# A three-stage kernel whose instruction order is planned by a program: how three planning rules are changed

## The chip, the cores and the metric

The kernel runs on one core of one Trainium2 chip. The metric is the device time of one execution in microseconds (us); the median of a few runs is compared. TensorE (PE in the profile) multiplies matrices into PSUM, VectorE (DVE) and ScalarE (ACT) work element by element, GpSimd (POOL) does a little, and SyncE (SP) issues most DMAs. Each engine executes its own instructions strictly in the order in which they stand, and waits at the first one whose inputs or buffers are not ready.

## The reference, cut to what matters

Three layers follow each other over 4 sequences of 768 positions: a chunked scan with decays (8 heads, 32 values, state of 16), a gated feed-forward layer (256 to 1536 to 256) behind an RMS norm, and a second one (256 to 1024 to 256) that mixes each position with the one before.

```python
cum = np.cumsum(la, axis=-1)                       # la = log(clip(a)), in a chunk
M = CB * np.exp(cum_i - cum_j) * causal            # CB = C @ B^T, the "scores"
y = M @ x + (C @ state) * np.exp(cum)
state = decay_full * state + sum_j(B_j x_j * decay_from_j)
...
xn = x / rms * rms_g
x = (silu(xn @ w_gate) * (xn @ w_val)) @ w_out     # silu(g) = g * sigmoid(g)
...
k = np.maximum(xk @ w_k, 0); out = sigmoid(xr @ w_r) * (k * k @ w_v)
```

## The kernel before, in words

Time is cut into 6 chunks (`NC`) of 128 positions (`P`), each with all 4 sequences (`NB`): 512 columns (`T`). Chunk 0 of the scan stands alone ahead of everything. Then, in tile `t`, the first feed-forward layer of chunk `t` (`ffn1`, 12 units of gate `g`, value `v`, product `hf`, contraction into `x2`) runs with the scan of chunk `t + 1` between its units, and the second layer (`ffn2`) of chunk `t - 1` follows. Every wide product is three matmuls of 512 columns on values split into a high and a low part (`mm3`, L615 to L617): ScalarE rounds the high part (`split`, L128) and VectorE subtracts it for the low part (L131). The weights arrive as 64-bit numbers and are turned into such pairs in `convert` during the first two tiles, by ScalarE (L255, L256, L276) and VectorE (L260, L265, L267, L277).

In the scan, the decay matrices `E` of chunks 0 and 1 are made on chip: `sums_e` gets the cumulated logs, the matmuls `cumt` (L338) turn them into `cum`, `spread_e` spreads them over a bank `Eb` (L346, L347) and ScalarE's `exp_e` takes 4 exponentials of 128 columns from each bank (L116). `scores` multiplies B and C into two banks `sc` (L441 for chunks 0 and 1 on rows 0 to 31 and 32 to 63 of the array, one half of the rows for each bank; L448 for chunk 2 on rows 0 to 15 and 32 to 47; L454, on all rows, for the later ones). `mask` (L473) multiplies `sc` with `E` on VectorE and so frees the banks. `y_two` (L515, L486, L492) makes the output and state of two sequences in two banks. The scans `la_scan` (L399) and `e_scan` (L408) prepare the decays for the state and for later chunks.

PSUM has eight banks: 2 of `pacc` (tag "acc"), 4 of `pmm` ("mm": `g`, `v`, `kp`, `ss`), 2 of `patt` ("at": `sc`, `y`, and `Eb` from chunk 1 on). The order in which instructions stand on each engine comes from `Order`: it plays the program through with a price for every instruction (`price`) and a model of the waits, always gives a free engine the earliest written instruction that `can` run, and `arrange` ties every instruction behind the one ahead of it on its engine. `can` asks whether a tile that is first touched here has its turn and a free buffer. `chains` are extra pairs "this before that". The prices set only the order: what an instruction takes on the chip is another matter.

Of the kernel before, what the change touches and what calls it, by code (L numbers as in the profile page):

```python
# [16 lines left out]
P = 128  # L17
# [50 lines left out]
def tile_kernel(ctx: ExitStack, tc, a_c, x_t, B_t, B_s, C_s, B_p, C_p, C_h, kc,  # L68
                w_gate, w_val, w_out, w_k, w_v, w_r, out):
    nc = tc.nc  # L70
    slots, chains = {}, []

    class Pool:
        def __init__(self, name, bufs, space=None):
# [253 lines left out]
    def sums_e(a_sb):  # L328
        nc.vector.memset(f32(sums), 0.0)
        ln = t2("ln")[:RE]  # L330
        tabled(out=ln, in_=a_sb[:RE], func=AF.Ln)
        nc.vector.tensor_tensor_scan(out=ln, data0=starts.rearrange("p h i -> p (h i)"), data1=ln, initial=0.0,
                                     op0=ALU.mult, op1=ALU.add)
        nc.vector.tensor_copy(sums[:RE], ln)
        nc.vector.tensor_tensor(out=sums[32:32 + RE], in0=ln, in1=f32(sums[:RE]), op=ALU.subtract)
        ps = patt.tile([P, T], F32, tag="at", name="cumt")[:, :4 * RE].rearrange("p (h r) -> p h r", h=4)
        for h in range(4):
            nc.tensor.matmul(ps[:, h], sums[:, h * P:(h + 1) * P], pick, start=True, stop=True)  # L338
        nc.vector.tensor_scalar(out=cum, in0=ps, scalar1=-1.0, scalar2=None, op0=ALU.mult)

    def spread_e(c, b):
        for half in range(2):
# [20 lines left out]
    def parity(c):  # L363
        return c == 2
# [62 lines left out]
    def scores(c, b):  # L427
        d = A[c]
        bank = []
        for _ in range(2):  # L430
            if c == 0:
                pool, tag = pacc, "acc"
            else:
                pool, tag = patt, "at"
            bank.append(pool.tile([P, T], F32, tag=tag, name="sc"))
        if plain(c):
            br, cr = d.pop(("Br", b)), d.pop(("Cr", b))
            for q in range(2):
                for half in range(2):
                    g = slice(32 * half, 32 * half + 32)  # L440
                    nc.tensor.matmul(bank[half][:, q * 256:(q + 1) * 256], br[g, q, :],  # L441
                                     cr[g, 2 * q:2 * q + 2, :].rearrange("p a i -> p (a i)"), start=True, stop=True)
        elif parity(c):
            br, cr = d.pop(("Br", b)), d.pop(("Cr", b))
            for p in range(4):
                for j in range(2):
                    g = slice(32 * j, 32 * j + N)
                    nc.tensor.matmul(bank[j][:, p * P:(p + 1) * P], br[g, p, :], cr[g, p, :], start=True, stop=True)  # L448
        else:
            bs, cs = d.pop(("Bs", b)), d.pop(("Cs", b))  # L450
            for half in range(2):
                for q in range(2):
                    p = 2 * half + q
                    nc.tensor.matmul(bank[half][:, q * 256:(q + 1) * 256], bs[:, p, :],  # L454
                                     cs[:, p, :, :].rearrange("p a i -> p (a i)"), start=True, stop=True)
        for half in range(2):
            d["sc", b, half] = bank[half]
        if plain(c) and c or parity(c):
            load_bc(c, b + 2)
# [49 lines left out]
    def y_two(c, b):  # L509
        d = A[c]  # L510
        y = [patt.tile([P, T], F32, tag="at", name="y") for _ in range(2)]
        for k in range(2):
            for half in range(2):
                g = slice(64 * half, 64 * half + 64)
                nc.tensor.matmul(y[half][:, k * P:(k + 1) * P], Sf[g, b + k].rearrange("p h d -> p (h d)"),  # L515
                                 d["Ch"][g, b + k, :], start=k == 0, stop=False, skip_group_check=True)
        for k in range(2):
            y_x(y, (k * P, k * P), c, b + k, False)
            if c + 1 < NC:
                d["up", b + k] = y[k][:, 2 * P:2 * P + 2 * D]  # L520
                y_st(d["up", b + k], c, b + k)
        if b == 0:
            d["yT"] = rp.tile([P, 2, T], F32, tag="yT", bufs=1, name="yT")
        for half in range(2):
            nc.scalar.copy(d["yT"][:, half, b * P:(b + 2) * P], y[half][:, :2 * P])
        for k in range(2):
            st_up(c, b + k)
            sf_up(c, b + k)
# [223 lines left out]
        w_load()  # L752
    first, second = steps(), steps()
    clip(a_sb)
    sums_e(a_sb)
    spread_e(0, 0)
    scores(0, 0)
    spread_e(0, 1)
    for b in range(NB):
        for half in range(2):  # L760
# [145 lines left out]
        held[t] = x2  # L906
    mix(NC - 1, held.pop(NC - 1), act_e, vec_e)
    ffn2(NC - 1, lambda *_: None)
    arrange(tc, list(nc.cur_bb.bb.instructions), slots, chains)

# [15 lines left out]
class Order:  # L928
    SIGNAL, LANDING, RATE = 90.0, 1900.0, 270.0

    def __init__(self, instructions, slots, chains):
        self.slots, self.ins = slots, []
        where = {}
        for i in instructions:
            kind = type(i).__name__
            if i.engine in ENGINES and kind not in ("BassTilePoolBoundary", "InstRegisterMove"):
                where[i.name] = len(self.ins)
                self.ins.append(i)
        n = len(self.ins)
        self.eng = [i.engine for i in self.ins]  # L940
        self.before = [set() for _ in range(n)]
        for a, b in ((where[a], where[b]) for a, b in chains):
            self.before[b].add(a)
        self.tiles, self.touch = [[] for _ in range(n)], {}
        writes, reads = {}, {}
        for k, i in enumerate(self.ins):
            rs, ws = ([self.region(a, slots) for a in s if hasattr(a, "bass_ap")] for s in (i.ins, i.outs))
            for name, r in rs + ws:
                if name in slots and name not in self.tiles[k]:
                    self.tiles[k].append(name)  # L950
                    self.touch.setdefault(name, []).append(k)
            for name, r in rs:
                self.meet(k, r, writes.get(name, ()))
            for name, r in ws:
                self.meet(k, r, writes.get(name, ()))
                self.meet(k, r, reads.get(name, ()))
            for store, them in ((writes, ws), (reads, rs)):
                for name, r in them:
                    if slots.get(name, ("",))[0] == "PSUM":
                        store = writes  # L960
                    store.setdefault(name, []).append((r, k))
        self.cost = [self.price(i) for i in self.ins]
# [22 lines left out]
    def price(self, i):  # L985
        kind, e = type(i).__name__, i.engine
        aps = [a for a in i.outs if hasattr(a, "bass_ap")]
        n = max([columns(a) for a in aps] or [1])
        if kind == "InstDMACopy":
            return (380.0 if e == SP_ else 100.0), 0.0, False  # L990
        if e == PE_:
            x = i.ins[0]
            if x.dtype == F32:
                part = 0.3 if aps[0].ap[0][1] <= 32 else 0.55 if x.ap[0][1] <= 64 else 1.0
                return 20 + 1.7 * n * part, 200.0, False
            return (228.5 if n >= T else max(n / 2.4 + 15, 45.0)), 180.0, False
        if e == ACT_:
            return (1280.0, 0.0, False) if kind == "InstLoadActFuncSet" else (75 + 0.88 * n, 70.0, False)
        two = kind == "InstTensorTensor" or getattr(i, "is_scalar_tensor_tensor", False)
        if e == POOL_:  # L1000
            return (100 + 2.3 * n, 50.0, True) if kind == "InstTensorTensor" else (100 + 0.5 * n, 50.0, False)
        if kind == "InstMemset":
            return 60.0, 30.0, False
        psum = any(self.slots.get(a.bass_ap.tensor.name, ("",))[0] == "PSUM" for a in i.ins if hasattr(a, "bass_ap"))
        if getattr(i, "is_tensor_tensor_scan", False):
            return 20 + 2.22 * n, 70.0, True
        return 75 + (1.03 if two or psum else 0.52) * n, 75.0, not psum

    def run(self):
# [20 lines left out]
        t, serial, order, held, holder = 0.0, 0, [], set(), None  # L1030

        def can(k):
            return all(m in held or m in first.get(k, ()) and rank[m] == turn[self.slots[m][1]]
                       and free[self.slots[m][1]] > 0 for m in self.tiles[k])

        def release(j):
            left[j] -= 1
# [70 lines left out]
        return t, order  # L1108


def arrange(tc, instructions, slots, chains):
    o = Order(instructions, slots, chains)
    _, order = o.run()
    last = {}
    for k in order:
        i = o.ins[k]
        if i.engine in last:
            tc.add_manual_dep(i, last[i.engine].name, mybir.DependencyInfo(
                mybir.DependencyClass.NoSync, mybir.DependencyReason.DATA), reason="order")
        last[i.engine] = i  # L1120
# [38 lines left out]
```

## Time and profile before

| what | value |
|---|---|
| median of 3 runs (lowest, highest) | 542.84 us (542.33, 543.45) |
| the profiled execution's own time | 542.75 us |
| its span, first to last instruction | 541.0 us |
| TensorE busy in the span | 530.0 us (98%) |
| VectorE busy | 403.1 us (75%) |
| ScalarE busy | 315.0 us (58%) |
| mean granted TensorE clock | 0.986 of full speed |

The 1.75 us between own time and span lie around the instructions. Matmuls overlap in the pipeline, so that a busy TensorE row is longer than the distance to the next matmul; distances between starts are the truer measure there, and on VectorE too, where a following instruction starts before the end that is shown.

### The profile page before, as it was taken

How to read it: one execution, taken by the hardware profiler on the slowest of the kernel's cores; microseconds unless marked ns; L12 is line 12 of the kernel's file. 1: busy time of each engine (PE TensorE's matmuls, PEld its weight loads, DVE VectorE, ACT ScalarE, POOL GpSimd, SP SyncE). 2: the span in 40 equal slices, each digit the busy share in tenths (PEclk: the TensorE clock that was granted, in tenths of full speed). 3: DMA queues.
4: the chain of work that ended last, by engine and by line, in shares of the span. 5: the costliest groups of instructions: out<-in, count | busy, mean ns of one | idle time of the engine just before them, and what ended most of it. 6: DMA issues, size and time to landing. Idle time of an engine off the chain costs nothing.

```text
span 541.0 us, 7496 instructions
## 1 busy us (share of the span) xinstructions
PE 530.0 (98%) x2831; PEld 421.4 (78%) x2831; DVE 403.1 (75%) x640; ACT 315.0 (58%) x546; POOL 14.4 (3%) x30
## 2 busy tenths in 40 slices
PE   8979999999999999999999999999999999999997
PEld 5646777787778888888888888888887888888885
DVE  5797889999999986596986597986454873335672
ACT  3998557954745864355774356774337662345562
POOL 4000000000002000001000001000000000000000
PEclk9987999999989999999999999999999999999999
DMA  8552456533426011316011315011000010000001
GB/s 261 157 179 93 170 166 220 199 89 113 131 59 184 32 41 39 117 43 184 29 39 40 117 44 171 1 40 39 1 0 2 1 39 1 0 0 1 18 22 39
DMA packets 21635, 42.20 MB, mean 78 GB/s; under 512 B 2064, under 2 KB 4880, under 8 KB 21600
## 3 DMA queue, kind: packets, MB, share of 16 engines
q1 hardware_dynamic: 19296, 33.34, 18.9%
q10 hardware_dynamic: 2304, 8.39, 4.8%
q8 instruction: 22, 0.36, 0.3%
q14 instruction: 13, 0.11, 0.1%
HBM read 38.38 MB, written 3.34 MB: 77 GB/s over the span
## 4 chain that ended last, share of the span: by engine, by line
PE 71%; DVE 2%; issue 0%; DVEq 0%
PE v L617 8%; PE v L616 8%; PE v L615 8%; PE x L616 5%; PE x L617 5%; PE x L615 5%; PE g L615 4%; PE g L617 4%; PE g L616 4%; PE kp L615 4%; PE kp L617 4%; PE kp L616 4%; PE y L486 1%; PE sc L454 1%; PE rps L617 1%; PE rps L616 1%
## 5 line engine op out<-in xcount | busy, mean ns | idle before, releaser
L646 DVE TENSOR_TENSOR hf<-sl,v 128x512 f32<-128x512 f32 x72 | 49.2, 684 | 53.9 <-PE v L617 49.8
L128 ACT CAST h<-hf 128x512 fp32r<-128x512 f32 x72 | 44.5, 619 | 69.3 <-DVE hf L646 64.8
L116 ACT ACTIVATE sl<-g 128x512 f32<-128x512 f32 x72 | 42.7, 594 | 48.3 <-PE g L617 48.3
L131 DVE TENSOR_TENSOR h<-hf,h 128x512 fp32r<-128x512 f32 x72 | 50.5, 703 | 23.7 <-ACT h L128 23.4
L615 PE MATMUL g<-xn,wgh 128*128 128x512 f32 x144 | 58.5, 408 | 0.3 <-ACT sl L116 0.3
L617 PE MATMUL v<-xn,wvh 128*128 128x512 f32 x144 | 57.8, 401 | 0.0
L616 PE MATMUL v<-xn,wvl 128*128 128x512 f32 x144 | 57.8, 401 | 0.0
L617 PE MATMUL g<-xn,wgh 128*128 128x512 f32 x144 | 57.2, 397 | 0.0
L616 PE MATMUL g<-xn,wgl 128*128 128x512 f32 x144 | 57.1, 397 | 0.0
L615 PE MATMUL v<-xn,wvh 128*128 128x512 f32 x144 | 57.1, 400 | 0.0
L615 PE MATMUL x<-h,woh 128*128 128x512 f32 x144 | 56.9, 395 | 0.0
L616 PE MATMUL x<-h,wol 128*128 128x512 f32 x144 | 56.9, 395 | 0.0
L617 PE MATMUL x<-h,woh 128*128 128x512 f32 x144 | 56.0, 393 | 0.0
L712 DVE TENSOR_TENSOR k<-rl 128x512 f32<-128x512 f32 x48 | 34.6, 724 | 15.3 <-ACT rl L711 15.0
L128 ACT CAST h<-k 128x512 fp32r<-128x512 f32 x48 | 29.6, 619 | 16.7 <-DVE k L712 16.5
L131 DVE TENSOR_TENSOR h<-k,h 128x512 fp32r<-128x512 f32 x48 | 32.6, 685 | 7.2 <-ACT h L128 6.7
L711 ACT ACTIVATE rl<-kp 128x512 f32<-128x512 f32 x48 | 28.6, 595 | 15.9 <-PE kp L617 15.3
L617 PE MATMUL v<-h,wvvh 128*128 128x512 f32 x96 | 37.8, 394 | 0.0
L617 PE MATMUL kp<-xm,wkh 128*128 128x512 f32 x96 | 37.8, 393 | 0.0
L615 PE MATMUL kp<-xm,wkh 128*128 128x512 f32 x96 | 37.7, 393 | 0.0
L616 PE MATMUL v<-h,wvvl 128*128 128x512 f32 x96 | 37.6, 392 | 0.0
L616 PE MATMUL kp<-xm,wkl 128*128 128x512 f32 x96 | 37.6, 392 | 0.0
(135 smaller groups left out, 1058.1 us busy)
## 6 DMA issues: line engine op xcount, KB each, us to landing
E<-la_r ACTq DMA_DIRECT2D x16, 512.0 KB
x<-in_x_t SPq DMA_DIRECT2D x6, 512.0 KB
wst<-in_w_gate SPq DMA_DIRECT2D x6, 512.0 KB
wst<-in_w_val SPq DMA_DIRECT2D x6, 512.0 KB
wst<-in_w_out SPq DMA_DIRECT2D x6, 512.0 KB
Br<-in_B_s SPq DMA_DIRECT2D x12, 256.0 KB
Cr<-in_C_s SPq DMA_DIRECT2D x12, 256.0 KB
out<-r SPq DMA_DIRECT2D x12, 256.0 KB
```

Of the source, the lines that this page charges most:

```text
L116: ins.append(lambda: nc.scalar.activation(out=out, in_=in_, func=func, **kw))
L128: nc.scalar.copy(x[:, 0, :], src)
L131: last[0] = le.tensor_tensor(out=x[:, 1, :], in0=src, in1=f32(x[:, 0, :]), op=ALU.subtract).ins
L454: nc.tensor.matmul(bank[half][:, q * 256:(q + 1) * 256], bs[:, p, :], cs[:, p, :, :].rearrange("p a i -> p (a i)"), start=True, stop=True)
L486: nc.tensor.matmul(y[half][32 * j:32 * j + 32, at[half]:at[half] + P], x[:, b, h * D:(h + 1) * D], m[:, h, :], start=start and at[half] == ...
L615: nc.tensor.matmul(ps, w[0][:, k, ws], x[:, 0, :], start=first, stop=False)
L616: nc.tensor.matmul(ps, w[1][:, k, ws], x[:, 0, :], start=False, stop=False)
L617: nc.tensor.matmul(ps, w[0][:, k, ws], x[:, 1, :], start=False, stop=last)
L646: nc.vector.tensor_mul(hf, sl, v)
L711: nc.scalar.activation(out=rl, in_=kp, func=AF.Relu)
L712: nc.vector.tensor_mul(k2, rl, rl)
```

## The change

Three rules of the planner are altered; the arithmetic stays.

1. **Groups.** For the products that can run at once on different rows of the array (`scores` of chunks 0 to 2 and the state products of `y_two`), the name of the first matmul is noted with the names of both banks. `Order` lets that matmul touch both banks, and `can` now checks several new tiles of one tag together: it waits until as many buffers are free.
2. **Column sums.** A chain puts the last `cumt` matmul ahead of the first matmul of `scores(0, 0)`.
3. **ScalarE's price.** Up to 128 columns cost 250 ns, wider ones 60 ns plus 0.94 ns a column (before: 75 plus 0.88), and the delay of the result 100 ns (before: 70).

```diff
-            nc.tensor.matmul(ps[:, h], sums[:, h * P:(h + 1) * P], pick, start=True, stop=True)
+            mm = nc.tensor.matmul(ps[:, h], sums[:, h * P:(h + 1) * P], pick, start=True, stop=True)
...
+        return mm.ins.name
...
-                    nc.tensor.matmul(bank[half][:, q * 256:(q + 1) * 256], br[g, q, :],
+                    mm = nc.tensor.matmul(bank[half][:, q * 256:(q + 1) * 256], br[g, q, :],
                                      cr[g, 2 * q:2 * q + 2, :].rearrange("p a i -> p (a i)"), start=True, stop=True)
+                    if q + half == 0:
+                        groups.append((mm.ins.name, [t.name for t in bank]))
...
+                if k + half == 0:
+                    groups.append((mm.ins.name, [t.name for t in y]))
...
-    sums_e(a_sb)
+    cumt = sums_e(a_sb)
     spread_e(0, 0)
     scores(0, 0)
+    chains.append((cumt, groups[0][0]))
...
-            for name, r in rs + ws:
+            for name in [name for name, _ in rs + ws] + groups.get(i.name, []):
...
-            return (1280.0, 0.0, False) if kind == "InstLoadActFuncSet" else (75 + 0.88 * n, 70.0, False)
+            return (1280.0, 0.0, False) if kind == "InstLoadActFuncSet" else ((60 + 0.94 * n if n > P else 250.0), 100.0, False)
...
         def can(k):
-            return all(m in held or m in first.get(k, ()) and rank[m] == turn[self.slots[m][1]]
-                       and free[self.slots[m][1]] > 0 for m in self.tiles[k])
+            new = {}
+            for m in sorted((m for m in self.tiles[k] if m not in held), key=rank.get):
+                tag = self.slots[m][1]
+                j = new[tag] = new.get(tag, -1) + 1
+                if m not in first.get(k, ()) or rank[m] != turn[tag] + j or free[tag] <= j:
+                    return False
+            return True
```

What stands on TensorE behind the 16 warm-up matmuls, first before and then after the change (`Eb` are banks of `spread_e`, `sc` those of the first scores):

```order
L346 MATMUL Eb_181<-before_85,eye_84 128x512
L346 LDWEIGHTS eye_84
L346 MATMUL Eb_184<-before_85,eye_84 128x512
L441 MATMUL sc_187<-Cr_144,Br_146 128x256
L441 MATMUL sc_188<-Cr_144,Br_146 128x256
L441 MATMUL sc_187<-Cr_144,Br_146 128x256
L441 MATMUL sc_188<-Cr_144,Br_146 128x256
L346 LDWEIGHTS eye_84
L346 MATMUL Eb_193<-before_85,eye_84 128x512
L346 LDWEIGHTS eye_84
L346 MATMUL Eb_196<-before_85,eye_84 128x512
L338 MATMUL cumt_175<-pick_76,sums_120 128x16 x4
```

```order
L347 MATMUL Eb_193<-before_85,eye_84 128x512
L347 LDWEIGHTS eye_84
L347 MATMUL Eb_196<-before_85,eye_84 128x512
L338 MATMUL cumt_175<-pick_76,sums_120 128x16 x4
L348 MATMUL Eb_181<-sums_120,pick_76 128x512
L348 MATMUL Eb_184<-sums_120,pick_76 128x512
L442 MATMUL sc_187<-Cr_144,Br_146 128x256
L442 MATMUL sc_188<-Cr_144,Br_146 128x256
```

The four `cumt` matmuls no longer stand behind the four products of `sc`.

On TensorE at the first units of tile 0, where the scores of chunk 1 begin (`sc_657`, `sc_658` are the two banks of its first sequence, `sc_717` one of the second), before and then after:

```order
L617 MATMUL g_554<-xn_388,wgh_106 128x512
L441 MATMUL sc_657<-Cr_435,Br_433 128x256 x2
L615 MATMUL v_539<-xn_388,wvh_108 128x512
L615 MATMUL v_561<-xn_388,wvh_108 128x512
L441 MATMUL sc_658<-Cr_435,Br_433 128x256 x2
L441 MATMUL sc_717<-Cr_439,Br_437 128x256
L616 MATMUL v_539<-xn_388,wvl_109 128x512
L617 MATMUL v_539<-xn_388,wvh_108 128x512
L616 MATMUL v_561<-xn_388,wvl_109 128x512
L617 MATMUL v_561<-xn_388,wvh_108 128x512
L441 MATMUL sc_717<-Cr_439,Br_437 128x256
L615 MATMUL g_575<-xn_383,wgh_106 128x512
```

```order
L623 MATMUL v_539<-xn_388,wvl_109 128x512
L624 MATMUL v_539<-xn_388,wvh_108 128x512
L623 MATMUL v_561<-xn_388,wvl_109 128x512
L624 MATMUL v_561<-xn_388,wvh_108 128x512
L442 MATMUL sc_657<-Cr_435,Br_433 128x256
L442 MATMUL sc_658<-Cr_435,Br_433 128x256
L442 MATMUL sc_657<-Cr_435,Br_433 128x256
L442 MATMUL sc_658<-Cr_435,Br_433 128x256
L622 MATMUL g_575<-xn_383,wgh_106 128x512
```

One group of four now stands behind all of `v_539` and `v_561`, where three pieces stood between them, and `sc_717` has moved behind the third unit.

On VectorE at the same place, from the merge of the third pair of weight blocks (`wt2_455`) to the first `hf`, before and then after:

```order
L267 SCALAR_TENSOR_TENSOR wt2_455<-wt2_455,wst4_416 128x1024
L464 TENSOR_TENSOR Bd_727<-Bt_449,E_493 128x128
L464 TENSOR_TENSOR Bd_810<-Bt_449,E_508 128x128
L473 TENSOR_TENSOR E_478<-sc_657,E_478 128x512
L277 TENSOR_TENSOR wvl_109<-wt2_455,wvh_108 128x2x256
L277 TENSOR_TENSOR wol_111<-wt2_455,woh_110 128x512
L399 SCALAR_TENSOR_TENSOR la_441<-la_441,lmask_99 128x516
L646 TENSOR_TENSOR hf_547<-sl_546,v_539 128x512
```

```order
L400 SCALAR_TENSOR_TENSOR la_441<-la_441,lmask_99 128x516
L277 TENSOR_TENSOR wvl_109<-wt2_455,wvh_108 128x2x256
L277 TENSOR_TENSOR wol_111<-wt2_455,woh_110 128x512
L404 TENSOR_TENSOR Ch_447<-Ch_447,la_441 128x512
L469 TENSOR_TENSOR Bd_727<-Bt_449,E_493 128x128
L469 TENSOR_TENSOR Bd_810<-Bt_449,E_508 128x128
L400 SCALAR_TENSOR_TENSOR la_671<-la_671,lmask_99 128x516
L469 TENSOR_TENSOR Bd_940<-Bt_449,E_523 128x128
L478 TENSOR_TENSOR E_478<-sc_657,E_478 128x512
L478 TENSOR_TENSOR E_478<-sc_658,E_478 128x512
L653 TENSOR_TENSOR hf_547<-sl_546,v_539 128x512
```

The product `Ch_447`, a second scan (`la_671`, of chunk 2), `Bd_940` and the second mask of `E_478` now stand ahead of the first `hf`; all four stood behind it.

## Rows read from the trace of the kernel before

**Rows 1.** Stages: length, busy PE, PEld, DVE, ACT, POOL, then clock, DMA share, GB/s

```profile
10.40:41.00 30.60, 25.35 (x185) 16.17 (x183) 24.61 (x48) 30.17 (x88) 1.65 (x4) 0.94 0.58 188
41.00:73.40 32.40, 32.27 (x118) 22.76 (x119) 25.65 (x35) 21.74 (x33) 0.00 (x0) 0.89 0.41 143
73.40:154.40 81.00, 80.37 (x513) 62.64 (x512) 79.51 (x120) 54.02 (x85) 0.10 (x1) 1.00 0.43 140
...
194.00:541.00 347.00, 343.08 (x1772) 280.87 (x1771) 229.47 (x368) 182.68 (x301) 4.35 (x4) 1.00 0.12 42
```

**Rows 2.** Timeline of VectorE: start, duration, idle before it and what ended it

```profile
42.17 0.69 DVE L473 TENSOR_TENSOR E<-sc,E 128x512 f32<-128x512 f32 x1 [1.40 <-PE sc L441]
51.97 0.69 DVE L646 TENSOR_TENSOR hf<-sl,v 128x512 f32<-128x512 f32 x1 [2.05 <-PE v L617]
59.20 0.69 DVE L646 TENSOR_TENSOR hf<-sl,v 128x512 f32<-128x512 f32 x1 [1.87 <-PE v L617]
73.48 0.69 DVE L646 TENSOR_TENSOR hf<-sl,v 128x512 f32<-128x512 f32 x1 [1.61 <-PE v L617]
```

**Rows 3.** VectorE and TensorE at 154 to 158 us, timeline

```profile
154.39 0.66 DVE L646 TENSOR_TENSOR hf<-sl,v 128x512 f32<-128x512 f32 x1
...
156.37 1.28 DVE L131 TENSOR_TENSOR h<-hf,h 128x512 fp32r<-128x512 f32 x2
...
157.16 0.39 PE L616 MATMUL x<-h,wol 128*128 128x512 f32 x1
```

**Rows 4.** TensorE at the start, timeline

```profile
7.52 0.60 PE L346 MATMUL Eb<-before,eye 128*128 128x512 bf16 x2
8.05 1.13 PE L441 MATMUL sc<-Cr,Br 32*128 32x256 f32 x8
9.12 0.60 PE L346 MATMUL Eb<-before,eye 128*128 128x512 bf16 x2
9.37 0.69 PE L338 MATMUL cumt<-pick,sums 128*128 128x16 f32 x4
```

**Rows 5.** VectorE at the start, timeline

```profile
7.23 0.68 DVE L335 TENSOR_TENSOR sums<-ln,sums 16x512 fp32r<-16x512 f32 x1
```

**Rows 6.** ScalarE: the first exponentials, and what follows the last ones

```profile
10.44 6.31 ACT L116 ACTIVATE E<-Eb,cum 128x128 f32<-128x128 f32 x24 [5.58 <-PE Eb L347]
...
43.04 1.28 ACT L115 ACT_TABLE_LOAD   x1
44.34 0.60 ACT L116 ACTIVATE sl<-g 128x512 f32<-128x512 f32 x1
```

**Rows 7.** VectorE at 39 to 46 us, timeline

```profile
39.14 1.23 DVE L267 SCALAR_TENSOR_TENSOR wt<-wt,wst 128x1024 int32<-128x1024 int32 x1
...
43.98 1.23 DVE L399 TENSOR_TENSOR_SCAN la<-la,lmask 128x516 f32<-128x516 f32 x1
45.12 0.66 DVE L646 TENSOR_TENSOR hf<-sl,v 128x512 f32<-128x512 f32 x1
45.70 0.69 DVE L403 TENSOR_TENSOR Ch<-Ch,la 128x512 f32<-128x512 f32 x1
```

**Rows 8.** TensorE from 41 to 54 us, timeline

```profile
41.01 1.13 PE L441 MATMUL sc<-Cr,Br 32*128 32x256 f32 x4 [0.19 <-ACT E L116]
...
46.82 0.79 PE L615 MATMUL g<-xn,wgh 128*128 128x512 f32 x1
...
51.70 0.40 PE L615 MATMUL x<-h,woh 128*128 128x512 f32 x1
...
53.10 0.40 PE L615 MATMUL g<-xn,wgh 128*128 128x512 f32 x1
```

**Rows 9.** A stage in that stretch, columns as in rows 1

```profile
46.00:48.00 2.00, 2.00 (x5) 1.16 (x5) 2.00 (x4) 2.00 (x4) 0.00 (x0) 0.50 0.22 66
```

**Rows 10.** One pair of the split scores on TensorE, timeline

```profile
70.33 0.69 PE L441 MATMUL sc<-Cr,Br 32*128 32x256 f32 x2
70.95 0.74 PE L615 MATMUL v<-xn,wvh 128*128 128x512 f32 x2
```

More of the change, by code (lines that the diff above doesn't have):

```diff
@@ L70, in tile_kernel @@
     nc = tc.nc
-    slots, chains = {}, []
+    slots, chains, groups = {}, [], []
     class Pool:
@@ L447, in scores @@
                     g = slice(32 * j, 32 * j + N)
-                    nc.tensor.matmul(bank[j][:, p * P:(p + 1) * P], br[g, p, :], cr[g, p, :], start=True, stop=True)
+                    mm = nc.tensor.matmul(bank[j][:, p * P:(p + 1) * P], br[g, p, :], cr[g, p, :], start=True, stop=True)
+                    if p + j == 0:
+                        groups.append((mm.ins.name, [t.name for t in bank]))
         else:
@@ L514, in y_two @@
                 g = slice(64 * half, 64 * half + 64)
-                nc.tensor.matmul(y[half][:, k * P:(k + 1) * P], Sf[g, b + k].rearrange("p h d -> p (h d)"),
+                mm = nc.tensor.matmul(y[half][:, k * P:(k + 1) * P], Sf[g, b + k].rearrange("p h d -> p (h d)"),
                                  d["Ch"][g, b + k, :], start=k == 0, stop=False, skip_group_check=True)
+                if k + half == 0:
+                    groups.append((mm.ins.name, [t.name for t in y]))
         for k in range(2):
@@ L908, in tile_kernel @@
     ffn2(NC - 1, lambda *_: None)
-    arrange(tc, list(nc.cur_bb.bb.instructions), slots, chains)
+    arrange(tc, list(nc.cur_bb.bb.instructions), slots, chains, groups)
 ENGINES = (mybir.EngineType.PE, mybir.EngineType.DVE, mybir.EngineType.Activation, mybir.EngineType.Pool,
@@ L929, with __init__ @@
     SIGNAL, LANDING, RATE = 90.0, 1900.0, 270.0
-    def __init__(self, instructions, slots, chains):
+    def __init__(self, instructions, slots, chains, groups):
         self.slots, self.ins = slots, []
+        groups = dict(groups)
         where = {}
@@ L1108, in run, with arrange @@
         return t, order
-def arrange(tc, instructions, slots, chains):
-    o = Order(instructions, slots, chains)
+def arrange(tc, instructions, slots, chains, groups):
+    o = Order(instructions, slots, chains, groups)
     _, order = o.run()
```

## The prediction

> **What bounds the kernel now.** I read the stages first [rows 1]. TensorE is busy nearly throughout, and from 194 us to the end it waits for nothing: of 347.0 us only 3.9 are left, nearly all behind the last matmul. A gain can thus only come from what happens before, and what is gained there stays. Ahead of 41 us ScalarE is the bound: 30.17 of 30.60 us busy. It works off the exponentials of chunks 0 and 1, and the first `silu` stands behind them and a table load [rows 6]. From 73.4 to 154.4 us VectorE is full: 79.51 of 81.00 us, 1.49 us idle. In between, from 41.0 to 73.4 us, VectorE idles 6.75 us. The timeline says where [rows 2]: four waits of 1.40, 2.05, 1.87 and 1.61 us, 6.93 together (the rows' gaps count a little more than the stage shows), all for TensorE.
>
> Where does VectorE's lateness reach TensorE? At 154.39 us VectorE turns to a `hf`, and the two low parts `h` that follow begin at 156.37; the first is done 0.6 us later, at 156.97, and TensorE's third matmul on that `h` precedes the row of 157.16 [rows 3]. So TensorE takes this product the moment VectorE has made it. Everything behind follows at full pace.
>
> **My measuring point is that `hf` at 154.39 us.** The order on VectorE differs before it, but the set of instructions ahead of it is the same in both orders, and behind it the engine's order is at first unchanged. The same work in the same durations means that this `hf` comes earlier by exactly the idle time that VectorE loses before it. The sum is a list of VectorE's idle times.
>
> **The column sums.** Before, four products of `sc` stand on TensorE ahead of `cumt`: they take it from 8.05 to 9.12, and `cumt` starts at 9.37 [rows 4]. Its input is ready at 7.23 + 0.68 = 7.91 [rows 5]. After the change four `Eb` matmuls stand there: two of them went from 7.52 to 8.05, so four reach to about 8.5, and `cumt` starts at 8.4 to 8.5, some 0.9 to 1.0 us earlier. `cum` and the first exponential at 10.44 [rows 6] move with it. The four products now stand behind the first two `Eb` sums; they end near 10.6, when the first four exponentials end too (0.263 us each, 6.31 over 24), so the first mask finds both. Two conversions of weights stand behind exponentials that they preceded, which moves VectorE's first masks forward too. ScalarE has 0.43 us of slack in the whole stage, so the shift arrives at the end: first `silu` at 43.25 to 43.35 where it was 44.34. Bounds: nothing, if a wait for a bank of `Eb` in the new order eats it, to 1.2. I take **1.0**; VectorE's work of this stage is moved by the same.
>
> **The first masks: 1.40 us of waiting.** In the new order VectorE finds other work here. With the merge of 39.14 [rows 7] ending near 39.2 (39.14 + 1.14 less the shift of about 1.05), the listed rows run: scan 1.14 (43.98 to 45.12), two subtractions and `Ch` 0.6 each (45.12 to 45.70 is 0.58), two `Bd` 0.4, second scan 1.14, `Bd` 0.2, two masks 1.2, and the first `hf` at 45.1. TensorE waits for both banks until the last exponential, 41.9 (before, 43.04 less 1.05), and is done with the four products at about 43.0 (1.07 us for all four, from rows 4), 0.9 before VectorE reaches the masks at 43.9. **Saves 1.4.** These scans and the `Ch` are work that stood later, so nothing is added to VectorE. The price is that `hf` stands behind them: 45.1, as before (45.12).
>
> **The third `hf`: 2.05 us.** TensorE's next unit needs a bank of "mm", freed by the first `silu` at 43.3 + 0.6 = 43.9. Before, the same unit began at 46.82 and the contraction behind it at 51.70 [rows 8]; 12 matmuls took 4.88 us since the clock stood at half there (0.50, [rows 9]), where 6 take 1.40 at full clock (51.70 to 53.10). The clock's fall followed TensorE's thin work from 41 us on, and that stays thin: a wait, four products, a wait. I assume one more such low stretch, about half as long as the one in rows 8 and 9: two of the 12 matmuls at 0.233, eight at 0.43 (the 12 of rows 8 took 0.41 on the mean, the last of them at full pace again), two at 0.233. The unit ends at 48.25, the contraction starts 3.45 us earlier than before. VectorE has four operations of 0.6 from its first `hf` at 45.1, this one included, ahead of the third, and reaches it at 47.6: a wait of 0.65. **Saves 1.4.**
>
> **The fourth and the sixth `hf`: 1.87 and 1.61 us.** VectorE has 8.15 us of work from the third `hf` on to the fourth (four merges of 1.14 as in rows 7, six operations of 0.6): 56.4. TensorE has 33 matmuls, 7.7 us, and one pair of scores at 0.62 (70.33 to 70.95, [rows 10]) with about 0.2 of changeover: 56.75. Wait 0.35, **saves 1.5**. To the sixth: VectorE 11.75 us (four merges, twelve operations of 0.6) and one wait for ScalarE that I put at 0.45 (its conversion stands behind a `silu` now), 68.95; TensorE 43 matmuls, 10.0 us, and three pieces of scores (one of 1.05, two of 0.62, each with 0.2), 2.9: 69.65. Wait 0.7, **saves 0.9**; the 0.45 is a new idle time.
>
> **From 73.4 to 154.4 us** I leave the 1.49 us as they are.
>
> **Sum:** 1.0 + 1.4 + 1.4 + 1.5 + 0.9 - 0.45 = 5.75 us. Off the profiled execution's own 542.75: **537.0 us** (the median is 542.84, 0.09 more).
>
> Does TensorE follow? It must be 5.75 us earlier at 157 us. It has 3.45 from the start. The scores of chunk 1 stood in nine pieces and stand in six now, those of chunk 2 in six and now in five; a piece less is worth at least 0.8 us, one pair and its changeover [rows 10]. That makes 3.45 + 3.3 = 6.7 or more: VectorE decides.
>
> **A rule against it.** What the rows show is that TensorE's clock stood at half (1.2 of 2.4 GHz) behind a thin stretch [rows 9], which cost the 12 matmuls of rows 8 some 2.1 us (4.88 less 2.8). The Trainium skill, "TensorE: Matmul & The Clock Gate", section "Why this matters for your kernels", says that idle gaps between bursts of matmuls bring the slower clock back; waiting for both banks makes such gaps. By that rule the time is the third rival's below. This trace agrees as far as rows 9 go.
>
> **The rivals.**
> 1. *VectorE's waits close further.* No low stretch at 44 us: the unit ends at 46.7, VectorE is the later one throughout, and all of 6.93 + 1.0 goes but the new 0.45: 7.5 us, 535.3. For it: less mixed work on TensorE there. Against: it still waits twice between 41 and 44 us. Chance 0.14.
> 2. *My forecast,* with its own range of 536.0 to 538.2. Chance 0.45.
> 3. *The clock falls once more.* Either the low stretch of the third `hf` lasts as long as before (1.3 us more), or TensorE's wait for the `h` of 157 us, now longer because TensorE is ahead of VectorE, is followed by one: 8 matmuls at 0.43 in place of 0.233, 1.55 us, at a place where nothing takes it back. One of them gives 538.3 to 538.6, both 539.9. Chance 0.24.
> 4. *The planner only reshuffles.* VectorE's idle times reappear elsewhere between 73 and 154 us, for instance at a `ms` or a conversion that now stands too early. Then the 5.75 are given back to within 1.1: 541.7 to 543.9. Against: the stage has 1.49 us of idle in 81 now, with similar neighbours. Chance 0.10.
> 5. *Slower: the moved scans wait for their loads.* Two scans now stand ahead of the first `hf`, and an engine waits in order. Each us that their input lands after about 42 us delays the first `hf`, and TensorE with it, at half clock. It decides from 6.85 us on (5.75 + 1.1), when the loads of chunk 2's decays land after 48.9. At 8 us late the time is 545.0. Against: the scan of chunk 1 ran at 43.98 without a wait in the trace [rows 2, 7], and the order on SyncE now puts all these loads ahead of the next weights. Chance 0.07.
>
> **Range and chances.** 0.2% of the median is 1.1 us, about what a measurement of this kernel can tell from no change. Cases 1 to 3 end below 541.7: 0.83 faster. Case 4 is no change, 0.10; case 5 slower, 0.07. For 8 in 10 the range reaches from 534.5 (case 1 with the bound of 1.2 and the new wait gone, 8.15 us) to 540.6 (case 3 with both, and the column sums mostly lost).
>
> **What would show it.** `cumt` near 8.4 and the first exponential near 9.5; the first `silu` near 43.3; on VectorE no wait ahead of the first masks, and waits under 1 us where rows 2 have 2.05, 1.87 and 1.61; the contraction near 48.3; the `hf` of 154.39 near 148.6 and TensorE waiting for its `h` there; every group of scores in one piece except those of the second and third sequences of chunk 1 and the first of chunk 2. I am wrong if TensorE, not VectorE, is late there, or if idle time grows between 73 and 149 us.

## The result, and the profile after

The changed kernel took 536.12 us (median of 4 runs, 535.15 to 536.48) against 542.59 us of before beside it (4 runs, 538.71 to 543.45): a ratio of 0.9892, 95% interval 0.9842 to 0.9941. Six later runs (e7 below) gave 536.44. The prediction was 537.0, its range 534.5 to 540.6. The profiled execution took 536.48 us, its span is 534.4.

One thing must be known to read any of these numbers. The runs of one kernel fall on levels that go with the mean granted clock of the run. Of 72 runs of before that stood beside the experiments, 22 had a mean clock of 0.992 or more and took 538.6 to 540.0 us; 40 had 0.984 to 0.987 and took 540.9 to 545.1; 10 had 0.979 to 0.981 and took 543.8 to 544.2. The profiled execution of before is of the middle level. Below, kernels are therefore compared by median and also at like clock.

The stages of the changed kernel, columns as in [rows 1]:

```profile
10.40:41.00 30.60, 24.94 (x189) 16.07 (x188) 26.46 (x49) 30.26 (x86) 1.65 (x4) 0.94 0.59 203
41.00:73.40 32.40, 31.62 (x131) 23.33 (x131) 29.78 (x43) 23.98 (x36) 0.00 (x0) 0.95 0.45 146
73.40:154.40 81.00, 77.97 (x517) 60.58 (x516) 79.72 (x120) 52.88 (x85) 0.11 (x1) 1.00 0.43 141
194.00:534.00 340.00, 336.52 (x1744) 275.48 (x1742) 223.63 (x358) 177.82 (x293) 4.24 (x4) 1.00 0.12 41
```

From 41.0 to 73.4 us VectorE now idles 2.62 us, where it idled 6.75, and the clock's mean there is 0.95 in place of 0.89. From 73.4 on VectorE is as full as before. Its timeline in the middle stretch, against [rows 2] and [rows 7]:

```profile
36.85 1.22 DVE L267 SCALAR_TENSOR_TENSOR wt<-wt,wst 128x1024 int32<-128x1024 int32 x1
...
42.64 1.28 DVE L478 TENSOR_TENSOR E<-sc,E 128x512 f32<-128x512 f32 x2
43.84 0.68 DVE L653 TENSOR_TENSOR hf<-sl,v 128x512 f32<-128x512 f32 x1
...
48.33 0.69 DVE L653 TENSOR_TENSOR hf<-sl,v 128x512 f32<-128x512 f32 x1 [1.80 <-PE v L624]
...
56.73 0.69 DVE L653 TENSOR_TENSOR hf<-sl,v 128x512 f32<-128x512 f32 x1
...
61.94 1.23 DVE L265 SCALAR_TENSOR_TENSOR wst<-wt,wst 128x1024 int32<-128x1024 int32 x1 [0.20 <-ACT wst L256]
...
69.46 0.69 DVE L653 TENSOR_TENSOR hf<-sl,v 128x512 f32<-128x512 f32 x1 [0.30 <-PE v L624]
```

The wait ahead of the first masks (42.64) is gone, the fourth `hf` waits for nothing, the sixth 0.30 us; the third still waits 1.80 us. The start and the contraction behind the first unit, against [rows 4], [rows 6] and [rows 8], from the timelines of TensorE and ScalarE:

```profile
7.19 1.04 PE L347 MATMUL Eb<-before,eye 128*128 128x512 bf16 x4
7.96 0.61 PE L338 MATMUL cumt<-pick,sums 128*128 128x16 f32 x4
...
48.06 0.39 PE L622 MATMUL x<-h,woh 128*128 128x512 f32 x1
...
8.94 5.26 ACT L116 ACTIVATE E<-Eb,cum 128x128 f32<-128x128 f32 x20 [4.08 <-PE Eb L348]
...
41.67 1.28 ACT L115 ACT_TABLE_LOAD   x1
42.97 0.60 ACT L116 ACTIVATE sl<-g 128x512 f32<-128x512 f32 x1
```

The place of [rows 3], VectorE and then TensorE:

```profile
147.74 0.68 DVE L653 TENSOR_TENSOR hf<-sl,v 128x512 f32<-128x512 f32 x1
...
149.74 1.29 DVE L131 TENSOR_TENSOR h<-hf,h 128x512 fp32r<-128x512 f32 x2
...
149.13 0.51 PE L622 MATMUL x<-h,woh 128*128 128x512 f32 x1 [1.21 <-ACT h L128]
...
150.48 0.50 PE L624 MATMUL x<-h,woh 128*128 128x512 f32 x1 [0.38 <-DVE h L131]
```

The `hf` of 154.39 us comes 6.65 us earlier, and the span is 6.6 us shorter. TensorE waits there for what ScalarE and VectorE make of it. So the place where lateness reaches the end was read rightly; what the experiments had to settle is where the 6.65 us come from.

### The profile page after: what moved, and what is told of

Same layout as the page of the kernel before. It is cut to its first block, busy times and chain, and to the rows that moved or that the text cites. A ratio compares the mean times of both kernels' runs of the same rounds, so it can differ in the third digit from the quotient of the medians.

```text
span 534.4 us, 7505 instructions
## 1 busy us (share of the span) xinstructions
PE 520.0 (97%) x2831; PEld 414.5 (78%) x2831; DVE 402.7 (75%) x640; ACT 314.3 (59%) x546; POOL 14.2 (3%) x30
## 4 chain that ended last, share of the span: by engine, by line
PE 71%; DVE 2%; issue 0%; DVEq 0%
PE v L624 8%; PE v L623 8%; PE v L622 8%; PE x L624 5%; PE x L623 5%; PE x L622 4%; PE g L622 4%; PE g L624 4%; PE g L623 4%; PE kp L622 4%; PE kp L624 4%; PE kp L623 4%; PE y L491 1%; PE sc L459 1%; PE rps L624 1%; PE rps L623 1%
## 5 line engine op out<-in xcount | busy, mean ns | idle before, releaser
L624 PE MATMUL v<-xn,wvh 128*128 128x512 f32 x144 | 56.6, 393 | 0.0
L622 PE MATMUL v<-xn,wvh 128*128 128x512 f32 x144 | 56.4, 395 | 0.0
```

The source lines that it names most:

```text
L622: nc.tensor.matmul(ps, w[0][:, k, ws], x[:, 0, :], start=first, stop=False)
L624: nc.tensor.matmul(ps, w[0][:, k, ws], x[:, 1, :], start=False, stop=last)
```

## The experiments

Theory A is the prediction's: the gain is idle time that VectorE loses ahead of that `hf`. Theory B: it is the unbroken pieces of scores on TensorE. Theory C: it is ScalarE's price alone. The clock theory came up when the levels showed: part of the gain is low stretches of the clock (stretches at half of the full clock) that the new order avoids or shortens.

All have the change's three parts on or off, or add work to it. "Clock" is the mean granted clock over the runs, lowest to highest. Ratios are to before beside them on one chip.

| run | groups, chain, price | median us (runs) | lowest to highest | clock | ratio, 95% interval |
|---|---|---|---|---|---|
| before | no, no, no | 542.87, 542.79, 541.92 (35, 17, 20) | 538.6 to 545.1 | 0.979 to 0.994 | |
| e1 | yes, no, no | 543.91 (12) | 541.3 to 546.6 | 0.986 to 0.993 | 1.0009 to 1.0062 |
| e2 | no, yes, no | 538.17 (12) | 537.5 to 543.7 | 0.979 to 0.994 | 0.9923 to 0.9989 |
| e3 | no, no, yes | 542.53 (12) | 539.5 to 544.0 | 0.982 to 0.994 | 0.9991 to 1.0044 |
| e4 | yes, yes, no | 541.38 (12) | 539.5 to 544.0 | 0.979 to 0.990 | 0.9966 to 1.0014 |
| e5 | yes, no, yes | 537.19 (6) | 535.8 to 537.7 | 0.990 to 0.995 | 0.9873 to 0.9935 |
| e6 | no, yes, yes | 542.44 (12) | 538.9 to 547.2 | 0.973 to 0.994 | 0.9966 to 1.0026 |
| e7 | the whole change | 536.44 (6) | 536.2 to 537.4 | 0.989 to 0.994 | 0.9873 to 0.9929 |
| e8 | whole, filled at three waits | 535.06 (6) | 534.6 to 535.8 | 0.999 to 1.000 | 0.9846 to 0.9901 |
| e9 | before, filled | 539.50 (12) | 538.4 to 544.2 | 0.983 to 1.000 | 0.9953 to 1.0016 |
| e10 | whole, filled at 25 to 29 us | 534.77 (6) | 534.3 to 537.2 | 0.997 to 1.000 | 0.9861 to 0.9937 |
| e11 | whole, filled at 40 and 43 us | 535.39 (6) | 534.7 to 535.6 | 0.993 to 0.996 | 0.9859 to 0.9936 |
| e12 | e8 and more on VectorE | 536.65 (9) | 536.1 to 537.3 | 0.999 to 1.000 | 0.9891 to 0.9949 |

The edits that switch a part off are one line each (the last is cut to the expression that differs):

```diff
 # no groups
-    arrange(tc, list(nc.cur_bb.bb.instructions), slots, chains, groups)
+    arrange(tc, list(nc.cur_bb.bb.instructions), slots, chains, [])
 # no chain
-    chains.append((cumt, groups[0][0]))
 # the old price
-    ((60 + 0.94 * n if n > P else 250.0), 100.0, False)
+    (75 + 0.88 * n, 70.0, False)
```

**One part alone, and two without the price.**

> The kernel before with the groups alone: products that run at once wait for all their banks; no chain for the column sums, ScalarE's old price. Theory A (the gain is VectorE's idle time ahead of its hf of about 154 us; TensorE is ahead and its pieces of scores cost nothing by themselves): VectorE's order puts the scan of decays and one more product ahead of the first masks, and one of the two masks behind the first hf, so the wait of 1.4 us there goes; the three others are bettered only in part: 539.5 to 541.3. Theory B (the unbroken pieces of scores on TensorE are the gain, 0.8 us a piece, about five pieces less): most of the whole gain, 536.5 to 538.5. Theory C (the gain is ScalarE's price, which decides what VectorE finds to do at 41 us): 541.5 to 543.5.

> The kernel before with the chain alone: column sums ahead of the first scores. VectorE's order is that of before, ScalarE's differs in one exponential. Theory A: exponentials start 1.0 us earlier, the whole of ScalarE's stage up to 41 us moves with them, and the four waits of VectorE keep their lengths, so that 0.9 to 1.1 us are left at the end: 541.4 to 541.9. Rival (ScalarE's lead is lost to the low stretch of TensorE's clock behind 41 us, which then only starts earlier against TensorE's work): 542.4 to 543.4. A longer gain than 1.3 us would say that the low stretch itself moved off the work.

> The kernel before with ScalarE's price alone. Theory C: VectorE's order has two scans, the product Ch and four small products ahead of the first two masks, as the whole change has, so the wait of 1.4 us goes and the third hf comes as in the whole change: 537.5 to 539.5. Theory A says the same of this wait, but the scores of chunk 1 stay in pieces and TensorE stays late for the fourth and the sixth hf: 538.5 to 540.5. Theory B (adjacency is the gain): 541.5 to 543.5.

> The whole change without ScalarE's new price: groups and chain alone. Theory A: what the groups give alone and 1.0 us of the chain, the two being independent: the time of the groups alone less 0.9 to 1.1 us, 538.4 to 540.3. Theory B: 535.5 to 537.0, the whole change's time, since the price would be worth nothing. Theory C: 540.5 to 542.5.

The groups alone made it slower by 0.1 to 0.6%, which no theory had; theory B is out by that and by e4. The price alone gave no measurable change, so theory C is out too, though the 541.38 of e4 lies in its range, as the median of e3 does in theory B's. Theory A missed all four medians, and at like clock it does no better: at 0.993 to 0.994 e1 took 541.3 to 541.9 and e3 539.5 and 539.9, against 538.6 to 540.0 of before at 0.992 to 0.994. So the groups alone lose 1.3 to 3.3 us there and the price alone gains nothing, where theory A had both some 1.6 to 4.4 us below the median of before. What failed was its forecast of the waits: with one part alone new ones come, as the profiles below show. The chain alone took 4.7 us off the median where 1.0 was expected. At like clock it is near that: seven of its twelve runs, at 0.993 to 0.994, took 537.5 to 538.3, some 1.1 to 1.7 us less than before. The rest of the 4.7 is that seven of twelve runs stood on this level where 22 of 72 did before; whether the chain brings that about or twelve runs fell so by chance is not shown.

With groups and chain but the old price (e4) the timelines of ScalarE and VectorE have

```profile
39.44 1.91 ACT L116 ACTIVATE E<-Eb,cum 128x128 f32<-128x128 f32 x7 [0.65 <-PE Eb L348]
...
41.89 0.69 DVE L277 TENSOR_TENSOR wvl<-wt,wvh 128x512 fp32r<-128x512 f32 x1 [1.70 <-ACT wvh L276]
```

and of e1

```profile
37.41 3.84 ACT L116 ACTIVATE E<-Eb,cum 128x128 f32<-128x128 f32 x14
...
41.79 0.69 DVE L277 TENSOR_TENSOR wvl<-wt,wvh 128x512 fp32r<-128x512 f32 x1 [1.18 <-ACT wvh L276]
```

The planner priced an exponential of 128 columns at 188 ns; it takes 263 ([rows 6], 6.31 over 24). ScalarE reached the cast of `wvh`, which stands behind such a run of exponentials, later than the planner thought, and VectorE, in order, stood still for it. In e1 fourteen exponentials stand unbroken ahead of the cast; at 75 ns too little each they make 1.05 of the 1.18 us. In e4 thirteen make 0.98 of the 1.70, and the 0.65 that ScalarE itself waits for an `Eb` make up nearly all the rest: TensorE was at half clock shortly before (0.50 from 34 to 36 us). So the wait fits two causes, the price and the clock; no run changed this place alone, and with the new price e7 still has 0.75 us here (below).

**The whole change less one part, and the whole again.**

> The whole change without the chain: groups and ScalarE's price. The runs so far fall on levels that go with the mean granted clock (before: 538.6 to 540 at 0.992, 542.4 to 543.4 at 0.986, 543.9 at 0.980), so the theories are told apart at like clock and by the median. Theory A (VectorE's idle time ahead of the hf of 154 us, and the groups need the price, since with the old price VectorE waited 1.2 and 1.7 us for ScalarE's conversions): the whole change's time and 1.0 us for the later column sums, 537.0 to 537.8 at a clock of 0.993 or more. Rival (the chain is most of the gain, as its median alone says, 4.7 us): 540.0 to 542.0.

> The whole change without the groups: chain and ScalarE's price. VectorE's order is that of the price alone. Theory A: the price alone at like clock (539.5 at 0.994) less 1.0 us for the earlier column sums: 538.3 to 538.8 at 0.993 or more, and a median of 540.0 to 541.7, since scores in pieces keep TensorE late. Rival (the groups give nothing, TensorE being ahead): the whole change's time, 535.5 to 536.8.

> The whole change once more, beside the others on one chip. If its four runs stand for it: 535.0 to 536.6, at a mean clock of 0.993 to 0.997. If it falls on levels as the kernel before does, with a second low stretch of the clock behind TensorE's wait for an h at 149 us or a longer one at 44 us, as the third rival of the prediction had it: some runs at 537.5 to 539.5 and a clock under 0.990.

Groups and price together (e5) give 5.6 us of the gain, though neither gives any alone; the rival, that the chain is most of the gain, is out. The chain adds 0.75 us (537.19 to 536.44), near the 1.0 expected, though the runs of the two overlap. Without the groups (e6) nothing is left in the median. At a clock of 0.993 to 0.994 its two runs took 538.9 and 539.8, near the 538.3 to 538.8 expected; eight of the other ten took 540.8 to 545.5, and the median lies above theory A's 540.0 to 541.7. Its profile shows a wait that neither before nor the whole change has. First ScalarE, then TensorE, timeline:

```profile
147.85 0.62 ACT L276 CAST wvvh<-wt 128x512 fp32r<-128x512 f32 x1 [1.84 <-DVE wt L267]
148.37 1.65 ACT L128 CAST xm<-xf 128x512 fp32r<-128x512 f32 x3
149.93 0.58 ACT L116 ACTIVATE sl<-g 128x512 f32<-128x512 f32 x1
...
150.57 0.79 PE L622 MATMUL g<-xn,wgh 128*128 128x512 f32 x1 [3.90 <-ACT sl L116]
```

A `silu` stands behind a cast that waits 1.84 us for VectorE and three more casts, and TensorE waits 3.90 us for the bank that this `silu` frees. The price alone (e3) has it at the same place, 3.56 us at 148.60. This is the fourth rival of the prediction, idle time that reappears behind 73 us, on TensorE rather than VectorE: it comes about with the price and without the groups. Each part of the change makes another order, and what an order is worth is decided by such single places; the effects do not add.

The whole change stayed narrow: all six runs of e7 within 1.2 us, four of them inside the 535.0 to 536.6 expected, where before spreads over 6.5. Its order is the same as in the profiled execution above, but its low stretch lay elsewhere. The stages of TensorE (busy time, clock, DMA share, GB/s), first of that execution:

```profile
29.00:31.00 2.00, 1.07 (x3) 0.75 0.36 107
31.00:33.00 2.00, 2.00 (x6) 0.50 0.00 0
33.00:35.00 2.00, 2.00 (x10) 0.90 0.26 23
...
45.00:47.00 2.00, 2.00 (x6) 0.50 0.30 80
```

and of e7:

```profile
29.00:31.00 2.00, 1.49 (x3) 0.50 0.41 121
31.00:33.00 2.00, 2.00 (x6) 0.50 0.01 2
33.00:35.00 2.00, 2.00 (x7) 0.50 0.18 11
...
45.00:47.00 2.00, 2.00 (x10) 1.00 0.60 194
```

The same instructions in the same order meet the low clock at 45 us in one execution and not in the other. VectorE's timeline of e7 shows what that does:

```profile
39.94 0.69 DVE L277 TENSOR_TENSOR wvl<-wt,wvh 128x512 fp32r<-128x512 f32 x1 [0.75 <-ACT wvh L276]
...
47.85 0.69 DVE L653 TENSOR_TENSOR hf<-sl,v 128x512 f32<-128x512 f32 x1 [0.24 <-PE v L624]
```

The third `hf` waits 0.24 us, not 1.80, but the longer low stretch from 29 to 36 us makes an `Eb` late: ScalarE waits 1.15 us for it, and VectorE then for ScalarE. The two executions took 536.17 and 536.48 us, both at a mean clock of 0.994: where the low stretch falls moves the waits. That the levels of before come about in the same way is likely, but not shown, since only one of its executions was profiled.

**TensorE's waits filled with unread products.** The order is made without them, and they are then put in front of three named instructions; their bank is one that the warm-up used. Two edits, cut:

```diff
+FILL = ((("Eb", 1, 1, 0), 16), (("Eb", 1, 3, 1), 3), ("g", 4))
...
+    for key, n in FILL:
+        fill[key] = [nc.tensor.matmul(warm, ones, ones.unsqueeze(1).broadcast_to([P, 4, P]), start=True, stop=True).ins
+                     for _ in range(n)]
...
-    for k in order:
-        i = o.ins[k]
+    for i in [i for k in order for i in fill.get(o.ins[k].name, []) + [o.ins[k]]]:
```

e8 fills all three places of the whole change, e10 the first alone, e11 the other two; e9 fills before with 16 and 2.

> The whole change with 23 more products of ones by ones on TensorE, whose result nothing reads, in three waits of TensorE: 16 ahead of the third Eb of chunk 1 (a wait of 4.0 us at 29.3), 3 ahead of the last Eb, 4 ahead of the g of 43.62; the order of all else is that of the whole change. Clock theory (the low stretches at 30 and 43.7 us follow TensorE's waits, and the second one costs the third hf some 1.3 us): granted clock of 1.00 from 30 to 47 us, contraction at 46.7 in place of 48.1, VectorE's wait for the third hf 0.4 in place of 1.8, 534.8 to 535.3 in nearly all runs. Rival (the low stretch at 43.7 comes from the products of scores, which use 32 rows, not from the wait): the clock stays at 1.00 at 30 us and falls at 44 us as before, 535.9 to 536.5.

> The kernel before with 18 unread products of ones by ones on TensorE in two of its waits (16 ahead of the third Eb of chunk 1, 2 ahead of the last Eb); all else in the order of before. It asks how much of the gain is order and how much the clock. If the low stretches of before at 44 to 51 us and at 153.6 follow from the wait near 29 us too, they go, the clock is 0.997 or more, and what is left between this and the whole change filled (535.1) is the order alone: 537.5 to 538.6. If those stretches come from the pieces of scores, which stand in front of both, the clock stays near 0.987 to 0.990 in most runs and the median near 542.

> The whole change with the 16 unread products ahead of the third Eb alone. Tells which of TensorE's waits costs: if the low stretch at 43.7 us comes from what stands right ahead of it (the wait of 0.8 us for a bank, and the scores), the clock is 0.997 and the time stays at 535.8 to 536.5. If the wait of 4 us at 25 to 29 us is the root of both, 534.8 to 535.3.

> The whole change with the 3 and the 4 unread products ahead of the last Eb and the g of 43.62, not the 16. If what stands right ahead of the low stretch of 43.7 us matters, this alone brings 534.8 to 535.5 at a clock of about 0.997, the stretch at 30 us staying without effect since ScalarE sets the pace there. If the wait at 25 to 29 us is the root, 535.9 to 536.5.

e8 came out near what the clock theory said. Its runs, 534.60 to 535.81, do not overlap those of e7 beside them, and it beats before by 1.0 to 1.5%. A stage of TensorE in e8, columns as above:

```profile
43.00:48.00 5.00, 5.00 (x23) 1.00 0.31 92
```

The timelines of e8, TensorE's contraction and then VectorE's third and fourth `hf`:

```profile
46.51 0.40 PE L625 MATMUL x<-h,woh 128*128 128x512 f32 x1
...
46.78 0.69 DVE L659 TENSOR_TENSOR hf<-sl,v 128x512 f32<-128x512 f32 x1 [0.35 <-PE v L629]
...
55.31 0.69 DVE L659 TENSOR_TENSOR hf<-sl,v 128x512 f32<-128x512 f32 x1
```

At full clock the contraction starts at 46.51, not 48.06, and the third `hf` waits 0.35 us, not 1.80. The medians of e10 and e11 lie within 0.4 us of that of e8, which is inside their spread, so which of the waits matters stays open: e10 kept the clock at 1.00 in three of its runs (534.3 to 534.5) but not in the others (535.1 at 0.998, 536.7 and 537.2 at 0.997).

e9 separates order from clock, but only in four of its twelve runs: the others stood at 0.983 to 0.995 and took 539.4 to 544.2, so its median of 539.50 lies in neither range expected. In its profiled execution (538.42 us) the clock stood at 1.00 from 10.4 us to the stage that ends at 533. VectorE's timeline of e9:

```profile
41.32 0.69 DVE L481 TENSOR_TENSOR E<-sc,E 128x512 f32<-128x512 f32 x1 [1.39 <-PE sc L445]
...
55.12 0.69 DVE L659 TENSOR_TENSOR hf<-sl,v 128x512 f32<-128x512 f32 x1 [0.74 <-ACT sl L118]
...
69.33 0.69 DVE L659 TENSOR_TENSOR hf<-sl,v 128x512 f32<-128x512 f32 x1 [1.60 <-PE v L629]
```

Of the four waits of [rows 2] those of 1.40 and 1.61 us are still there at full clock. The 2.05 of the third `hf` is gone, and of the 1.87 of the fourth 0.74 is left, now for ScalarE: the rest of these two went with the half clock. In four runs at a clock of 1.000 e9 took 538.4 to 538.7; the filled whole change at 1.000 took 534.3 to 535.3 (e8, e10). So the order by itself is worth 3.1 to 4.4 us. On VectorE it is 3.65 us at the `hf` of 154.39, which e9 has at 150.21 (shown further below) and e8 at 146.56:

```profile
146.56 0.68 DVE L659 TENSOR_TENSOR hf<-sl,v 128x512 f32<-128x512 f32 x1
```

The other 2.0 to 3.3 of the 6.4 us are low clock: it costs before some 4 us at its median (542.8 less 538.6), the whole change 1.4 to 1.7 (536.4 less 535.1 and 534.8).

**More work on VectorE.**

```diff
+    fill["hf"] = [nc.vector.tensor_tensor(out=junk, in0=wide, in1=wide, op=ALU.add).ins
+                  for _ in range(4)]
```

> The filled whole change with four more operations on VectorE (ones and ones added, 128x256, never read) ahead of the hf of the tenth unit of chunk 0, at about 105 us: 1.3 to 1.4 us of work, at half of 0.6 us and a little for each. Theory A (VectorE decides up to the hf of 149 us): all of it comes out at the end, 536.3 to 536.6. Rival (TensorE decides, VectorE has slack by then): 535.0 to 535.4, the time of the filled change.

The timeline of VectorE in e12:

```profile
85.95 1.80 DVE L796 TENSOR_TENSOR junk<-ones 128x256 f32<-128x256 f32 x4
87.67 0.68 DVE L659 TENSOR_TENSOR hf<-sl,v 128x512 f32<-128x512 f32 x1
...
147.81 0.68 DVE L659 TENSOR_TENSOR hf<-sl,v 128x512 f32<-128x512 f32 x1
```

That `hf` stands at 87.67 us, not at 105 as I had put it, and the four took 1.72 us (85.95 to 87.67), not 1.3 to 1.4. Of these the median gained 1.59 (535.06 to 536.65); between the two profiled executions the `hf` near 147 us moved by 1.25 (146.56 to 147.81) and the span by 1.3 (533.2 to 534.5). So VectorE decides there, as theory A says: of what it gains or loses ahead of 149 us at least some seven tenths come out at the end.

## Why the prediction was right, point by point

**The bound and the measuring point** held: 6.65 us on VectorE, 6.6 on the span, and e12 shows the coupling by itself.

**The terms** against VectorE's timeline of the two profiled executions:

| term | predicted us | measured us |
|---|---|---|
| column sums, what VectorE is earlier by at the merge of 39.14 | 1.0 | 2.29 (36.85) |
| first masks | 1.4 | 1.40 |
| third hf | 1.4 | 0.25 (2.05 to 1.80) |
| fourth hf | 1.5 | 1.87 |
| sixth hf | 0.9 | 1.31 (1.61 to 0.30) |
| new waits for ScalarE | -0.45 | about -0.5 (2.62 less 1.80 and 0.30, gaps of every kind; 0.20 at 61.94 the longest named) |
| sum | 5.75 | 6.6 |

Two terms were mis-sized and nearly cancel. The column sums brought VectorE 2.29 us, not 1.0. Not all of this is the change: the first `Eb` of [rows 4], whose place did not change, began at 7.52 in before, and e9, with the order of before, has from the timelines of TensorE and VectorE

```profile
6.71 0.60 PE L349 MATMUL Eb<-before,eye 128*128 128x512 bf16 x2
...
38.30 1.23 DVE L269 SCALAR_TENSOR_TENSOR wt<-wt,wst 128x1024 int32<-128x1024 int32 x1
```

The same merge stands at 38.30 there, so 0.84 of the 2.29 us is a late start of the profiled execution of before, and 1.45 is left for the change. That the sum came within 0.9 us is in part luck. The third `hf` then got 0.25 and not 1.4, because VectorE stood there at 46.53 (48.33 less 1.80) and not at 47.6, while TensorE's contraction came at 48.06, near the 48.25 forecast. With the fourth and the sixth the lean was the same: VectorE's waits closed further than I said, toward the first rival, whose condition, no low stretch at 44 us, e8 meets: 535.06 against its 535.3. (e7 meets it too and took 536.17 in its profiled execution, for it has the longer low stretch at 29 to 36 us.)

**TensorE ahead of VectorE** held: 3.64 us from the contraction (51.70 to 48.06) against 3.45, and it waits 1.21 and 0.38 us for its `h` at 149 us.

**What I did not see** is that two of the four waits that I counted belong to the clock. I took the low stretch of [rows 9] for half as long after the change, which the profiled execution shows (45 to 47 us); but it is no property of the order, since e7 has none there. The 537.0 stands for a typical run, in which the low clock of before is in part avoided too, not for a price of the order alone, which is 3.1 to 4.4 us.

**The third rival** had a low stretch behind TensorE's wait at 149 us and put it at 1.55 us "at a place where nothing takes it back". The stretch did not come; the stage of 73.4 to 154.4 us has a clock of 1.00, and so has the next, to 194 us. The price was wrong too. Before has half clock from 154 to 157 us, e9 with the same order full clock. In before the `hf` stands at 154.39 [rows 3], in e9 at 150.21, and the first `kp` behind it on TensorE follows. The stage of TensorE and the timelines, of before and then of e9:

```profile
154.00:157.00 3.00, 3.00 (x9) 0.50 0.15 42
...
168.17 0.39 PE L615 MATMUL kp<-xm,wkh 128*128 128x512 f32 x1
```

```profile
154.00:157.00 3.00, 3.00 (x15) 1.00 0.33 111
...
150.21 0.67 DVE L659 TENSOR_TENSOR hf<-sl,v 128x512 f32<-128x512 f32 x1
...
163.83 0.39 PE L625 MATMUL kp<-xm,wkh 128*128 128x512 f32 x1
```

These are 13.78 us with the low stretch and 13.62 without: it cost 0.16 us, since TensorE has slack against VectorE there (in e9 it waits 0.67 us for its `h`).

The Trainium skill, "TensorE: Matmul & The Clock Gate", section "Why this matters for your kernels", says that idle gaps between bursts of matmuls bring the slower clock back. e8 agrees, where filling the gaps kept the clock at 0.999 to 1.000 in all six runs; e9 does in four of its twelve. The low stretch of before at 44 us does not show such a gap, so the prediction's word that the trace agrees rests on the low clock alone. A stage of before, columns as in [rows 1]:

```profile
42.00:44.00 2.00, 1.88 (x10) 1.02 (x9) 1.83 (x4) 1.98 (x4) 0.00 (x0) 1.00 1.01 369
```

TensorE is busy 1.88 of the 2.00 us ahead of that stretch. What sets it off stays open.

**The fourth rival** did not come about in the whole change (1.28 us of VectorE idle from 73.4 to 154.4 us, 1.49 before), but e3 and e6 show its like at 150 us. **The fifth** did not: the two scans run without a wait.

## What to carry to other kernels

Price a planner's operations from the trace before judging its other rules: the groups lost time with the old price and took 5.3 us off the median with the new one (542.53 to 537.19). A part tried alone says little of the whole when an order is remade; compare at like granted clock, or fill the tensor engine's waits in both kernels, so that the clock is out of the comparison. And where an engine is late in one execution, ask if another execution of the same order shows that wait too.

## What the runs showed that was not expected

The same kernel stands on levels up to 5 us apart that go with the mean granted clock, and the low stretches of two executions of one order fall at other places. Sixteen unread products in one wait of 4 us kept the clock at 1.00 in three of six runs and gave the lowest median here, 534.77 us, though not clearly below that of e8. And a low stretch is not worth a fixed price: at 45 us it made the third `hf` wait 1.80 and not 0.35 us (e8) or 0.24 (e7), at 154 us it cost 0.16 us.
